# Experts' rows as 16-bit planes, packed by slot and transposed by DMA; low parts of expert weights on VectorE

## The chip, the cores and the metric

One core of a Trainium2 chip runs the whole program. The metric is device microseconds (us) of one execution, the median of a few runs. The core's engines are TensorE (PE in the rows; PEld is its weight load), VectorE (DVE), ScalarE (ACT), GpSimd (POOL) and SyncE (SP), which only issues DMAs here. Each engine works through its own instructions in a fixed order and waits where an operand is not there.

## The reference

A linear attention with a decaying state is followed by a gated two-matrix product and then by a mixture of experts. Only the last part is touched by the change, together with the step that hands rows to it.

```python
def _moe_ref(x, w1, w2, w3, w_out):            # 3072 tokens, 384 -> 1024 -> 384
    return ((x @ w1) * (x @ w2) @ w3) @ w_out

def _moe2_ref(x, w_gate, w_noise, noise, w1, w2):   # 8 experts, 384 -> 1024 -> 384
    logits = x @ w_gate
    noisy_logits = logits + np.log1p(np.exp(x @ w_noise)) * noise
    top2 = np.argpartition(-noisy_logits, 2, axis=1)[:, :2]
    ...                                        # softmax over the two
    for e in range(E):
        for k in range(2):
            mask = top2[:, k] == e
            h = np.maximum(x[mask] @ w1[e], 0.0)
            out[mask] += top2_w[mask, k, None] * (h @ w2[e])
```

## The kernel before

**Stages.** Up to about 110 us the weights of the dense part are folded and split. From there to about 470 us, twelve groups of two 128-token chunks go through attention and the dense part. From about 470 us to the end the eight experts follow one another. All matrix products use operands split into a high part (fp32r) and a low part (the rest), and take three matmuls each: high by high, high by low, low by high (`mm3`, L170 to L172).

**Rows and slots.** `mo_out` (L530 to L537) copies a chunk's 128 x 384 result from PSUM to the tile `xo` and writes it to the DRAM tensor `x2d` ("x_rows" in the rows). The gate (`gate_top`, `gate_put`) gives each token two slots of the DRAM table `slots`. An expert has 800 slots, in seven pieces: six of 128 rows and one of 32. The first four pieces are the first half (512 rows), the other three the second half (288 rows). `load_idx` (L718) reads an expert's slots into the tile `ti`, `gather` (L730) fetches the rows of a piece by an indirect DMA on GpSimd's queue into the tile `xg` (the 32 rows into `xgt`).

**Transposes.** The first matmul of an expert wants its rows with the 384 features on the partitions. `tr(e, hf)` (L734 to L742) makes that on TensorE: for each of three feature blocks, one transpose per piece (L739) into a PSUM bank, then `split` (L123, L124) casts the bank to the high part `XTh` on ScalarE and subtracts on VectorE to the low part `XTl`. A half of four pieces takes 12 transposes, one of three pieces takes 9.

**Weights.** `load_e` (L696) brings half of a weight matrix (768 KB) from DRAM to `raw` or `raww`; `split_e` (L699 to L709) casts a quarter on ScalarE to `WAh` or `WBh` and subtracts it to the low part `WAl` or `WBl`. The subtraction is on VectorE for experts 0 and 1 and on GpSimd from expert 2 on.

**Products.** `mm1(hf, ff)` makes eight blocks of the hidden layer per half (9 matmuls each), evicted by ScalarE (L754) and VectorE (L755). `mm2(e, j)` makes the output rows of a piece (24 matmuls, or 16 at L777 for the 32 rows), scales them on ScalarE (L772) and adds them to `out` by an indirect DMA on GpSimd's queue (L782).

**Order.** VectorE runs in the order in which the program is written (`manual_schedule`). On the other engines a scheduler may move an instruction ahead, except where `keep_in_program_order` stands. In the steady stretch, the second half of expert e also contains the weight quarters of expert e + 1 and both of its `tr`. At the last group of chunks (`g == NGRP - 1`) the first half of expert 0 begins before the gate of the last four chunks is done: its four pieces are gathered from the rows that stand so far (slots of 512 rows are held for that), and its `tr(0, 0)` stands ahead of the last piece of the dense part, of which VectorE still has to make the low part `pl` (L521). The gate's last chain (`LZ`, `g_t` to `g_si`) runs beside `mm1` of expert 0, and `tr(0, 1)` stands in the middle of the fourth `mm2` of expert 0.

Of the kernel before, what the change touches and what calls it, by code (L numbers as in the profile page):

```python
# [18 lines left out]
P = 128  # L19
# [52 lines left out]
def tile_kernel(ctx: ExitStack, tc: tile.TileContext, dt, nat, w3t, wout, w1, w2, e1, e2, cf, ci, out):  # L72
# [425 lines left out]

    def mo_ab(g, fp, m):
# [31 lines left out]
    def mo_out(g):  # L531
        for tt in range(2):
            t = 2 * g + tt
            dve.tensor_copy(out=LZ[:, t, :], in_=bX[tt][:, DM:XW])
            xo = work.tile([P, DM], F32, name="xo")
            act.copy(out=xo, in_=bX[tt][:, :DM])
            act.dma_start(out=x2d[DUMP + t * P:DUMP + P + t * P], in_=xo)  # L537
# [110 lines left out]
    def fill_table():  # L648
        ti = ic("init").rearrange("p (j t) -> p j t", t=2)
        tv = table.rearrange("(r s) t -> r s t", s=CAP)  # L650
        with nc.allow_non_contiguous_dma("table rows"):
# [5 lines left out]
            out=x2d[:DUMP].rearrange("(a p) d -> p a d", p=P), in_=zeros[:, None, :].to_broadcast([P, NT, DM])))  # L657
# [13 lines left out]
    def open_a():  # L671
# [3 lines left out]
        XT["t"] = EP["a"].tile([P, DM], F32, name="xgt")  # L675
        pool.memset(XT["t"], 0.0)
# [10 lines left out]
    def open_b():  # L687
        EP["b"] = ctx.enter_context(tc.tile_pool(name="epb", bufs=1, side="right"))
        open_h(EP["b"], 1)

    def load_e(e, m, i):
# [4 lines left out]
        sp.dma_start(out=rw, in_=(e1, e2)[m][e, :, 1536 * i:1536 * i + 1536])  # L696
        RW[e, m, i] = rw

    def split_e(e, m, i, on=pool):  # L699
# [5 lines left out]
        if e == 1:  # L705

            tc.keep_in_program_order(cast)
            on = dve
        on.tensor_tensor(out=l, in0=src, in1=f(h), op=OP.subtract)  # L709

    def load_idx(e, hf, r):
        TI[e, hf] = EP["a"].tile([P, (TA, TB + 1)[hf], 2], I32, name=f"ti{hf}", bufs=2)
        for o, n, w, j in (((0, TA, TPT, 0),), ((HOLD, TB, TPT, 0), (CAP - TPL, 1, TPL, TB)))[hf]:
            if isinstance(r, int):
                v = table[e * CAPT + r * CAP + o:e * CAPT + r * CAP + o + w * n]
            else:
                v = table[bass.ds(r * CAP + (e * CAPT + o), w * n)]
            sp.dma_start(out=TI[e, hf][:w, j:j + n].rearrange("p j t -> p (j t)"),  # L718
                         in_=v.rearrange("(p j) t -> p (j t)", p=w))
# [8 lines left out]
    def gather(e, j, rows=NROW):  # L728
        XG[e, j] = EP["a"].tile([P, DM], F32, name="xg", bufs=NT - 1) if j < NT - 1 else XT["t"]
# [12 lines left out]

    MB, MC, AD = (bA, bB, bK), [1], [-1]

# [14 lines left out]
    def mm2(e, j, mid=None):  # L759
# [4 lines left out]
        y = EP["a"].tile([P, DM], F32, name="ye", bufs=5)  # L764
# [31 lines left out]
    def second_half(e, r, early=True):  # L796

        nx = e + 1 < E
        if nx:
            for i in range(2):  # L800
# [231 lines left out]
```

## Time and profile before

| | |
|---|---|
| Median of 3 runs | 936.07 us (935.48 to 936.13) |
| The profiled execution | 935.5 us, its span in the trace 933.6 us |
| TensorE busy | 905.8 us (97%) |
| VectorE, ScalarE, GpSimd busy | 447.8, 423.4, 330.4 us |
| Transposes for the experts | 168, 21 per expert |
| DMA moved | 111.66 MB, mean 120 GB/s |

Each execution has some 2 us outside its span. The page's slices and the windows of the trace show which engine is busy when; the waits show who made TensorE wait; the timelines show the places where an operand comes late.

### The profile page before, as it was taken

The page shows a single profiled execution, that of the slowest core. Times are in us where ns is not written, and L with a number is a line of the kernel's source. Part 1 is how long each engine was busy: PE and PEld are TensorE (multiplying, and loading weights), DVE is VectorE, ACT ScalarE, POOL GpSimd, SP SyncE. Part 2 cuts the span into 40 slices and gives each one's busy share as a digit, 9 for nine tenths or more (in the row PEclk, how much of TensorE's full clock was granted, in tenths as well). Part 3 has the DMA queues.
Part 4 walks back from the last instruction along what each step waited for, and adds up shares of the span by engine and source line. Part 5 has one row for each costly group of instructions (what it writes and reads, how often), then busy time and mean ns, then how long its engine had stood idle before and what let it go on. Part 6 is the DMA issues. An engine that isn't in the chain of part 4 may idle for free.

```text
span 933.6 us, 17851 instructions
## 1 busy us (share of the span) xinstructions
PE 905.8 (97%) x7235; PEld 842.0 (90%) x7235; DVE 447.8 (48%) x1126; ACT 423.4 (45%) x875; POOL 330.4 (35%) x267
## 2 busy tenths in 40 slices
PE   8888899999999999999999999999999999999994
PEld 6778799999999999999989989899998989989894
DVE  5878875856756666655363451322313123131320
ACT  6877555456455545544351442434323343342420
POOL 2100111041141231230406626655546565555422
PEclk9999999999999999999999999999999999999998
DMA  9936577254353352400231635344162533614112
GB/s 356 405 121 226 187 80 216 89 141 159 105 156 128 117 147 81 119 19 19 84 121 39 158 118 164 59 145 89 40 169 62 161 62 94 140 29 105 18 21 37
DMA packets 52718, 111.66 MB, mean 120 GB/s; under 512 B 18064, under 2 KB 32656, under 8 KB 52624
## 3 DMA queue, kind: packets, MB, share of 16 engines
q1 hardware_dynamic: 37008, 85.98, 29.3%
q0 software_dynamic: 12160, 19.72, 12.0%
q10 hardware_dynamic: 3456, 4.72, 1.4%
q8 instruction: 58, 0.95, 0.4%
q14 instruction: 36, 0.29, 0.1%
HBM read 88.12 MB, written 22.27 MB: 118 GB/s over the span
## 4 chain that ended last, share of the span: by engine, by line
PE 87%; DVE 6%; ACT 3%; DMA 1%; issue 1%; POOL 0%; ACTq 0%; POOLq 0%; SPq 0%; DVEq 0%
PE pb L170 26%; PE pb L171 25%; PE pb L172 25%; PE pb L308 4%; PE pb L248 2%; PE pb L739 2%; PE pb L777 1%; PE pb L269 1%; PE pb L258 1%; DVE cvz L154 1%; ACT top L145 1%; DMA raw<-w 1%; ACT am L241 1%; DMA raw<-e 0%; PE pb L374 0%
## 5 line engine op out<-in xcount | busy, mean ns | idle before, releaser
L170 PE MATMUL pb<-XTh,WAh 128*128 128x512 f32 (+1 forms) x384 | 133.3, 348 | 0.0
L171 PE MATMUL pb<-XTl,WAh 128*128 128x512 f32 (+1 forms) x384 | 131.8, 343 | 0.0
L170 PE MATMUL pb<-WBh,HH 128*128 128x384 f32 x384 | 130.9, 341 | 0.0
L172 PE MATMUL pb<-XTh,WAl 128*128 128x512 f32 (+1 forms) x384 | 130.7, 343 | 0.0
L172 PE MATMUL pb<-WBh,HH 128*128 128x384 f32 x384 | 129.6, 337 | 0.0
L171 PE MATMUL pb<-WBl,HH 128*128 128x384 f32 x384 | 129.5, 337 | 0.0
L755 DVE SCALAR_TENSOR_TENSOR HH<-pb,HH 128x256 fp32r<-128x256 f32 (+1 forms) x128 | 71.3, 558 | 116.0 <-ACT HH L754 116.0
L782 POOL DMA_INDIRECT out<-ye,ti x56 | 87.3, 1559 | 107.5 <-ACT ye L772 94.3
L754 ACT ACTIVATE HH<-pb 128x256 fp32r<-128x256 f32 (+1 forms) x128 | 62.9, 493 | 124.7 <-PE pb L172 123.6
L642 POOL DMA_INDIRECT slots<-g_sc,g_si x48 | 52.4, 1091 | 159.4 <-DVE g_si L641 82.4
L772 ACT ACTIVATE ye<-pb,ti 128x384 f32<-128x384 f32 x48 | 28.0, 583 | 145.4 <-PE pb L172 129.7
L124 DVE TENSOR_TENSOR XTl<-pb,XTh 128x512 fp32r<-128x512 f32 (+1 forms) x48 | 25.2, 569 | 130.4 <-ACT XTh L123 130.4
L228 POOL TENSOR_TENSOR rku<-nrk 128x384 f32<-128x384 f32 x21 | 21.9, 1041 | 184.1 <-DVE cc L235 79.8
L170 PE MATMUL pb<-xh,WAh 128*128 128x256 f32 x288 | 82.0, 285 | 3.6 <-DVE W1l L124 3.1
L170 PE MATMUL pb<-xh,WBh 128*128 128x256 f32 x288 | 81.4, 283 | 1.6 <-ACT WAh L156 1.1
L171 PE MATMUL pb<-xl,WAh 128*128 128x256 f32 x288 | 82.0, 285 | 0.9 <-DVE xl L315 0.9
L172 PE MATMUL pb<-xh,WAl 128*128 128x256 f32 x288 | 82.0, 285 | 0.0
L172 PE MATMUL pb<-xh,WBl 128*128 128x256 f32 x288 | 81.4, 283 | 0.3 <-DVE WBl L161 0.3
L171 PE MATMUL pb<-xl,WBh 128*128 128x256 f32 x288 | 81.4, 283 | 0.0
L170 PEld LDWEIGHTS pb<-XTh,WAh 128*128 128x128 f32 x384 | 72.2, 188 | 9.6 <-DVE HH L755 1.5
L171 PEld LDWEIGHTS pb<-XTl,WAh 128*128 128x128 f32 x384 | 72.2, 188 | 8.0
L172 PEld LDWEIGHTS pb<-XTh,WAl 128*128 128x128 f32 x384 | 71.7, 188 | 8.2
(174 smaller groups left out, 2191.9 us busy)
## 6 DMA issues: line engine op xcount, KB each, us to landing
dtc<-dt SPq DMA_DIRECT2D x24, 772.0 KB, 5.0
raw<-e SPq DMA_DIRECT2D x18, 768.0 KB, 6.6
raww<-e SPq DMA_DIRECT2D x14, 768.0 KB, 4.4
nrk<-nat SPq DMA_DIRECT2D x24, 384.0 KB, 5.2
rawf<-w3t SPq DMA_DIRECT2D x16, 512.0 KB, 7.3
nv<-nat SPq DMA_DIRECT2D x24, 256.0 KB, 3.4
raw<-w SPq DMA_DIRECT2D x8, 768.0 KB, 4.9
out<-zeros SPq DMA_DIRECT2D x9, 576.0 KB, 4.5
```

The costliest lines, as they stand in the source:

```text
L124: (on or dve).tensor_tensor(out=l, in0=src, in1=f(h), op=OP.subtract)
L170: pe.matmul(o, wh, xh, start=start, stop=False)
L171: pe.matmul(o, wh, xl, start=False, stop=False)
L172: pe.matmul(o, wl, xh, start=False, stop=stop)
L228: on.tensor_tensor(out=t, in0=RK[j][:, :DM], in1=RK[j][:, DM:], op=OP.mult)
L248: pe.matmul(bST[hb][:, P * a:P * a + P], KT[j][q, a].rearrange("p s i -> p (s i)"), RT[j][q, a].rearrange("p s i -> p (s i)"), start=True, ...
L308: pe.matmul(o, lt, rh, start=st, stop=en, tile_position=tp)
L642: ins = pool.indirect_dma_start(out=table, out_offset=bass.IndirectOffsetOnAxis(ap=si[:, i, k:k + 1], axis=0), in_=SC[:, i, k, :], in_offs ...
L754: act.activation(out=Hh[hf][:, ff], in_=bank[:, :n], func=AF.Relu)
L755: dve.scalar_tensor_tensor(Hl[hf][:, ff], bank[:, :n], 0.0, f(Hh[hf][:, ff]), op0=OP.max, op1=OP.subtract)
L772: act.activation(out=y[:n], in_=bank[:n], func=AF.Copy, scale=wt)
L782: ins = pool.indirect_dma_start(out=out, out_offset=bass.IndirectOffsetOnAxis(ap=ti(e, j)[:, 0:1], axis=0), in_=y[:n], in_offset=None, com ...
```

## The change

Rows are written to `x2d` as two planes of 16-bit halves: for each token the 384 low halves, then the 384 high halves. `mo_out` makes the planes in its copy, which now moves 768 two-byte numbers in place of 384 four-byte ones. `gather` fetches such rows. A new function `turn(e, hf)`, on SyncE's queue, writes each gathered piece to a DRAM tensor `rows` (packed by slot, the two planes of a row one after the other) and then issues one DMA transpose from there to a tile `XTx` (`XTa` for expert 0), whose columns are read as 32-bit numbers again. `tr` becomes a cast on ScalarE and a subtraction on VectorE from that tile. Only the second half of expert 0 keeps its transposes on TensorE (`tr_pe`), after copies on VectorE that join the planes (`join`). All subtractions in `split_e` are on VectorE. Loads of weights and slots keep their written order on SyncE's queue. There are three slot tiles of each kind in place of two, seven `xg`, and six `ye`.

```diff
-    x2d = nc.dram_tensor("x2_rows", [NROW, DM], F32, kind="Internal").ap()
+    x2d = nc.dram_tensor("x2_rows", [NROW, 2 * DM], U16, kind="Internal").ap()
+    rows = nc.dram_tensor("expert_rows", [2, 2 * CAP, DM], U16, kind="Internal").ap()
...
-            act.copy(out=xo, in_=bX[tt][:, :DM])
+            act.copy(out=halves(xo), in_=bX[tt][:, :DM].bitcast(U16).rearrange("p (d t) -> p t d", t=2))
...
     def load_e(e, m, i):
...
-        sp.dma_start(out=rw, in_=(e1, e2)[m][e, :, 1536 * i:1536 * i + 1536])
+        tc.keep_in_program_order(sp.dma_start(out=rw, in_=(e1, e2)[m][e, :, 1536 * i:1536 * i + 1536]))
-    def split_e(e, m, i, on=pool):
+    def split_e(e, m, i):
...
-        if e == 1:
+        if e:
             tc.keep_in_program_order(cast)
-            on = dve
-        on.tensor_tensor(out=l, in0=src, in1=f(h), op=OP.subtract)
+        dve.tensor_tensor(out=l, in0=src, in1=f(h), op=OP.subtract)
...
+    def turn(e, hf):
+        for j in range(TA) if hf == 0 else range(TA, NT):
+            tc.keep_in_program_order(sp.dma_start(
+                out=rows[e % 2, 2 * TPT * j:2 * TPT * j + 2 * rows_of(j)].rearrange("(p t) d -> p (t d)", t=2),
+                in_=XG[e, j][:rows_of(j)]))
+        a = 2 * hf * NAB[0]
+        s = slice(a, a + 2 * NAB[hf])
+        tc.keep_in_program_order(sp.dma_start_transpose(out=XT["x"].bitcast(U16)[:, :, s], in_=rows[e % 2, s]))
     def tr(e, hf):
-        n = NAB[hf]
+        s = slice(hf * NAB[0], hf * NAB[0] + NAB[hf])
         for db in range(3):
-            bank = PB[4 + db]
-            for j in range(TA) if hf == 0 else range(TA, NT):
-                o = TPT * (j - hf * TA)
-                pe.transpose(bank[:, o:o + P], XG[e, j][:, P * db:P * db + P], ident)
-            s = slice(hf * NAB[0], hf * NAB[0] + n)
-            split(XT["h"][:, db, s], XT["l"][:, db, s], bank[:, :n])
+            x, h = XT["x"][:, db, s], XT["h"][:, db, s]
+            tc.keep_in_program_order(act.copy(out=h, in_=x))
+            dve.tensor_tensor(out=XT["l"][:, db, s], in0=x, in1=f(h), op=OP.subtract)
...
     def first_half(e, r):
         if e + 1 < E:
             need(e + 1, 0, r)
             need(e + 1, 1, r)
+            for i in range(2):
+                load_e(e + 1, 0, i)
         for ff in range(8):
             mm1(0, ff)
+            if ff in (3, 6) and e + 1 < E:
+                turn(e + 1, ff // 6)
+            if e == 1 and ff == 3:
+                tr(1, 1)
...
+            if g == NGRP - 1 and i == 7:
+                turn(0, 0)
             if g == NGRP - 1 and i == 11:
                 tr(0, 0)
...
-        mm2(0, j, (lambda: tr(0, 1)) if j == TA - 1 else None)
+        mm2(0, j, tr_pe if j == TA - 1 else None)
...
+    turn(1, 0)
+    turn(1, 1)
...
-        if j < NT - 1:
-            tr(1, j - TA)
+        if j == NT - 2:
+            tr(1, 0)
```

On SyncE's queue, where the first half of expert 0 is fetched, the slots of its four pieces (`ti_5911`) were followed by weight loads alone. This is before:

```order
L718 DMA ti_5911<-slots 128x8
L696 DMA raw_6080<-e 128x1536
L696 DMA raw_6082<-e 128x1536
L696 DMA raww<-e 128x1536 x2
L929 TENSOR_LOAD rounds
L929 ISA x2
L718 DMA ti_6352<-slots 128x4
```

The same place after the change:

```order
L720 DMA ti_5910<-slots 128x8
L701 DMA raw_5963<-e 128x1536
L738 DMA expert_rows<-xg 128x768 x4
L743 DMA_TRANSPOSE XTa<-expert_rows 128x3x1024
L701 DMA raw_6086<-e 128x1536
L965 TENSOR_LOAD rounds
L965 ISA x2
L720 DMA ti_6345<-slots 128x4
L720 DMA ti_6345<-slots 32x2
L701 DMA raww<-e 128x1536 x2
```

(`rounds` holds how many rounds of slots each expert needs.) Four writes and the transpose now stand between the two weight loads of expert 0, and the two loads for expert 1 (`raww`) moved behind the slots of expert 0's second half.

On ScalarE, after the last group's copies, the transposed rows of expert 0 are cast (`XTh`), and the rows of the last two chunks are copied (`xo`). Before:

```order
L123 CAST XTh<-pb_70 128x512
L514 CAST ph<-pp 128x512
L123 CAST XTh<-pb_71 128x512
L123 CAST XTh<-pb_72 128x512
L704 CAST WBh<-raw_6082 128x768 x2
L536 COPY xo<-pb_68 128x384
L537 DMA x_rows<-xo 128x384
L536 COPY xo<-pb_69 128x384
L552 ACTIVATE g_t<-g_t 128x32
```

After:

```order
L518 CAST ph<-pp 128x512
L749 CAST XTh<-XTa 128x512 x3
L708 CAST WBh<-raw_6086 128x768 x2
L540 COPY xo<-pb_68 128x768
L781 ACTIVATE HH_5860<-pb_66 128x512
L541 DMA x_rows<-xo 128x768
L540 COPY xo<-pb_69 128x768
L556 ACTIVATE g_t<-g_t 128x32
```

The first eviction of `mm1` (`HH`) now stands ahead of the gate's first function (`g_t`), and the copies are of 768 numbers.

On VectorE the place of the low part `pl` is the same in both: behind the three subtractions for expert 0. After the change they read the DMA's tile:

```order
L515 TENSOR_TENSOR pp<-ac,pb_67 128x512
L750 TENSOR_TENSOR XTl<-XTa,XTh 128x512 x3
L525 TENSOR_TENSOR pl<-pp,ph 128x512
L538 COPY LZ<-pb_68 128x16
L538 COPY LZ<-pb_69 128x16
L555 TENSOR_SCALAR g_t<-LZ 128x32
```

Before, the three subtractions were separate rows that read the banks `pb_70` to `pb_72`; nothing else moved there.

## Rows read from the trace of the kernel before

**Rows 1.** Page, part 1: busy us, share of the span, instructions.

```profile
PE 905.8 (97%) x7235; PEld 842.0 (90%) x7235; DVE 447.8 (48%) x1126; ACT 423.4 (45%) x875; POOL 330.4 (35%) x267
```

**Rows 2.** Windows: stretch, us; busy (count) PE, PEld, DVE, ACT, POOL; clock; DMA.

```profile
110.00:470.00 360.00, 357.66 (x3789) 346.38 (x3788) 223.90 (x627) 181.41 (x407) 87.10 (x83) 1.00 0.41 112
536.00:922.00 386.00, 385.49 (x2252) 352.91 (x2250) 106.78 (x234) 138.62 (x253) 202.44 (x137) 1.00 0.39 92
```

**Rows 3.** Waits of PE from 110 us on: total us, times, longest.

```profile
PE pb L171 <- DVE xl L315: 0.9, 1, 0.9
```

**Rows 4.** Chain that ended last, experts 1 and 2: start us, us, what.

```profile
584.54 1.31 PE pb L739 x12
590.02 0.98 PE pb L739 x9
...
640.00 1.31 PE pb L739 x12
```

**Rows 5.** Timeline of POOL, last of four gathers for expert 0's first half.

```profile
464.45 0.95 POOL L730 DMA_INDIRECT xg<-x_rows,ti  x1 [0.30 <-issue]
```

**Rows 6.** DMA: landing of those four gathers; issues over the whole span.

```profile
DMA to landing us min/median/max: 3.1/3.3/3.8
...
raww<-e SPq DMA_DIRECT2D x14, 768.0 KB, 4.4
...
x_rows<-xo ACTq DMA_DIRECT2D x24, 192.0 KB, 1.9
...
slots<-cit SPq DMA_DIRECT2D x1, 128.0 KB, 7.8
```

**Rows 7.** Timeline of PE where expert 0 begins: start us, us.

```profile
473.82 0.43 PE L170 MATMUL pb<-W1h,ph 128*128 128x400 f32 x1
...
476.84 0.45 PE L172 MATMUL pb<-W1h,pl 128*128 128x400 f32 x1
...
478.41 0.39 PE L170 MATMUL pb<-XTh,WAh 128*128 128x512 f32 x1
478.64 0.39 PE L171 MATMUL pb<-XTl,WAh 128*128 128x512 f32 x1
```

**Rows 8.** Timelines of ACT and DVE at the same place.

```profile
473.27 0.59 ACT L123 CAST XTh<-pb 128x512 fp32r<-128x512 f32 x1 [1.44 <-issue]
...
478.15 0.47 ACT L536 COPY xo<-pb 128x384 f32<-128x384 f32 x1
...
484.82 0.60 ACT L754 ACTIVATE HH<-pb 128x512 fp32r<-128x512 f32 x1 [0.94 <-PE pb L172]
...
478.61 0.17 DVE L534 COPY LZ<-pb 128x16 f32<-128x16 f32 x1 [0.55 <-PE pb L172]
...
485.26 0.68 DVE L755 SCALAR_TENSOR_TENSOR HH<-pb,HH 128x512 fp32r<-128x512 f32 x1
```

**Rows 9.** Expert 0's second half: last gather, first transpose; gathers' landing from 529 to 541 us.

```profile
507.35 0.87 POOL L730 DMA_INDIRECT xgt<-x_rows,ti  x1 [0.30 <-issue]
...
510.39 0.38 PE L739 MATMUL pb<-cft,xg 128*128 128x128 f32 x2
...
DMA to landing us min/median/max: 5.4/6.1/6.7
```

**Rows 10.** Expert 1: last gather of its first half, first matmul.

```profile
514.32 0.96 POOL L730 DMA_INDIRECT xg<-x_rows,ti  x1 [0.30 <-issue]
...
535.15 0.48 PE L170 MATMUL pb<-XTh,WAh 128*128 128x512 f32 x1
```

**Rows 11.** Windows, columns as in rows 2: a wait of PE at 67 us, and after.

```profile
67.00:70.00 3.00, 0.06 (x1) 0.00 (x0) 2.28 (x5) 1.94 (x5) 0.77 (x2) 1.00 0.55 173
70.00:73.40 3.40, 3.20 (x15) 3.20 (x16) 3.06 (x7) 2.74 (x6) 0.00 (x0) 0.50 0.56 191
```

**Rows 12.** Instructions on `raww`: ns min, median, max; first and last start.

```profile
L704 ACT CAST WAh<-raww x28: 817/832/869, 527.8 to 840.1; 128x768 fp32r<-128x768 f32 x28
...
L709 DVE TENSOR_TENSOR WAl<-raww,WAh x4: 934/954/959, 528.7 to 537.9; 128x768 fp32r<-128x768 f32 x4
```

More of the change, by code (lines that the diff above doesn't have):

```diff
@@ L497, in tile_kernel, with halves @@
     PH, PL, AC, LOWP = {}, {}, {}, []
+    def halves(x):
+        return x.rearrange("p (t d) -> p t d", t=2)
     def mo_ab(g, fp, m):
@@ L534, in mo_out @@
             dve.tensor_copy(out=LZ[:, t, :], in_=bX[tt][:, DM:XW])
-            xo = work.tile([P, DM], F32, name="xo")
-            act.copy(out=xo, in_=bX[tt][:, :DM])
+            xo = work.tile([P, 2 * DM], U16, name="xo")
+            act.copy(out=halves(xo), in_=bX[tt][:, :DM].bitcast(U16).rearrange("p (d t) -> p t d", t=2))
             act.dma_start(out=x2d[DUMP + t * P:DUMP + P + t * P], in_=xo)
@@ L656, in fill_table @@
         tc.keep_in_program_order(sp.dma_start(
-            out=x2d[:DUMP].rearrange("(a p) d -> p a d", p=P), in_=zeros[:, None, :].to_broadcast([P, NT, DM])))
+            out=x2d[:DUMP].rearrange("(a p) d -> p a d", p=P), in_=zeros.bitcast(U16)[:, None, :].to_broadcast([P, NT, 2 * DM])))
     def fill_out(i):
@@ L689, in open_b @@
         open_h(EP["b"], 1)
+        XT["x"] = EP["b"].tile([P, 3, CAP], F32, name="XTx")
     def load_e(e, m, i):
@@ L717, in load_idx @@
                 v = table[bass.ds(r * CAP + (e * CAPT + o), w * n)]
-            sp.dma_start(out=TI[e, hf][:w, j:j + n].rearrange("p j t -> p (j t)"),
-                         in_=v.rearrange("(p j) t -> p (j t)", p=w))
+            tc.keep_in_program_order(sp.dma_start(out=TI[e, hf][:w, j:j + n].rearrange("p j t -> p (j t)"),
+                                                  in_=v.rearrange("(p j) t -> p (j t)", p=w)))
     def rows_of(j):
@@ L728, in gather, with join, tr_pe @@
     def gather(e, j, rows=NROW):
-        XG[e, j] = EP["a"].tile([P, DM], F32, name="xg", bufs=NT - 1) if j < NT - 1 else XT["t"]
+        XG[e, j] = EP["b" if e else "a"].tile([P, 2 * DM], U16, name="xg", bufs=NXG)
         pool.indirect_dma_start(out=XG[e, j][:rows_of(j)], out_offset=None, in_=x2d[:rows],
                                 in_offset=bass.IndirectOffsetOnAxis(ap=ti(e, j)[:, 0:1], axis=0))
-    def tr(e, hf):
-        n = NAB[hf]
+    def turn(e, hf):
[6 more added lines that the diff above has]
+        tc.keep_in_program_order(sp.dma_start_transpose(out=XT["x"].bitcast(U16)[:, :, s], in_=rows[e % 2, s]))
+    def tr(e, hf):
+        s = slice(hf * NAB[0], hf * NAB[0] + NAB[hf])
+        for db in range(3):
+            x, h = XT["x"][:, db, s], XT["h"][:, db, s]
+            tc.keep_in_program_order(act.copy(out=h, in_=x))
+            dve.tensor_tensor(out=XT["l"][:, db, s], in0=x, in1=f(h), op=OP.subtract)
+    def join(j):
+        x = EP["a"].tile([P, DM], F32, name="xg", bufs=NXG)
+        dve.tensor_copy(out=x[:rows_of(j)].bitcast(U16).rearrange("p (d t) -> p t d", t=2),
+                        in_=halves(XG[0, j][:rows_of(j)]))
+        XG[0, j] = x
+    def tr_pe():
+        for j in range(TA, NT):
+            join(j)
+        s = slice(NAB[0], NAB[0] + NAB[1])
         for db in range(3):
             bank = PB[4 + db]
-            for j in range(TA) if hf == 0 else range(TA, NT):
-                o = TPT * (j - hf * TA)
-                pe.transpose(bank[:, o:o + P], XG[e, j][:, P * db:P * db + P], ident)
-            s = slice(hf * NAB[0], hf * NAB[0] + n)
-            split(XT["h"][:, db, s], XT["l"][:, db, s], bank[:, :n])
+            for j in range(TA, NT):
+                n, o = rows_of(j), TPT * (j - TA)
+                pe.transpose(bank[:, o:o + n], XG[0, j][:n, P * db:P * db + P], ident[:n, :n])
+            split(XT["h"][:, db, s], XT["l"][:, db, s], bank[:, :NAB[1]])
     MB, MC, AD = (bA, bB, bK), [1], [-1]
+    NXG = 7
     def mm1(hf, ff, banks=None):
@@ L798, in second_half @@
         nx = e + 1 < E
-        if nx:
-            for i in range(2):
-                load_e(e + 1, 0, i)
         for ff in range(8):
@@ L809, in second_half @@
                 split_e(e + 1, 0, j)
-            if nx and j in (4, 5):
-                tr(e + 1, j - 4)
+            if nx and j in (3, 5):
+                tr(e + 1, j // 5)
         if nx:
@@ L920, in one_expert @@
         for hf in range(2):
+            turn(e, hf)
             tr(e, hf)
```

14 lines of the change are left out of this document (7 added, 7 removed).

## The prediction

> **What bounds the kernel now.** I read the page's busy times first: TensorE is busy for 905.8 us of the span of 933.6 us, and no other engine for half of it [rows 1]. The windows then show where. From 110 to 470 us it is busy for 357.7 of 360 us, and in the experts' steady stretch, 536 to 922 us, for 385.5 of 386 us at full clock, with VectorE at 106.8 us [rows 2]. The waits agree: from 110 us on TensorE was made to wait three times only, 0.9 us at the longest [rows 3]. So from 110 us on the time is the sum of TensorE's work. What is taken off it is gained whole, and any wait that the change puts ahead of it is paid whole.
>
> **The transposes removed.** The chain gives 1.31 us for the 12 transposes of a first half and 0.98 us for the 9 of a second half, 109 ns each [rows 4]. Expert 0 loses 12, experts 1 to 7 lose 21 each: 159 in all, 159 x 0.109 = **17.3 us off TensorE**. The 9 of expert 0's second half stay. An expert's period is 640.00 - 584.54 = 55.46 us [rows 4], and should be 55.46 - 2.29 = 53.2 us.
>
> **The price of a DMA transpose.** The trace has none, so I bound D, the time of the one for 1,024 x 384 two-byte numbers (786 KB). From below: as many bytes as a weight load of 768 KB, 4.4 us [rows 6]. From above: a DMA in small pieces. The table fill of 128 KB goes out as 4,096 pieces of 32 bytes and lands after 7.8 us, 1.9 ns a piece [rows 6]. If the transpose moves 128 numbers of a row at a time (its shape is 3 blocks of 128 columns), it has 3,072 pieces: 5.9 us. In pieces of 32 bytes it would have 24,576: 47 us. I take 6.5 us, near the piece count of whole blocks and the load of equal size, with a little for the weight load beside it. The second half's (576 rows) takes 0.56 of that.
>
> The Trainium skill, "DMA: Bandwidth & Descriptors", section "Latency and other measured facts", gives 261 GB/s for a DMA transpose; my estimate from that page, with the 2 us of fixed cost that it states for any DMA, is D = 5.0 us. No run here shows it yet. With it the first wait below would be 1.3 us and the whole 1.5 us shorter.
>
> **Steady stretch: hidden.** For experts 2 to 7 `turn` is issued in the first half of the expert before, and its result is wanted after that expert's fourth `mm2`, more than 35 us later. Both transposes take 1.56 D = 10 us and the six writes that matter 1.9 us each [rows 6], so this cover holds for D up to about 25 us. `turn` on SyncE's queue has the next `raw` loads behind it, which wait for the 32-row matmuls of the same expert anyway. GpSimd loses its 48 subtractions; VectorE gets them at 0.954 us [rows 12], 8 per expert, 46 us more in a stretch of 386 us where it has 106.8 [rows 2]: 40% busy, at the places where expert 1 had them on VectorE before. I charge nothing. `xo` copies grow from 0.47 us to about 0.83 us, as a cast of 768 numbers takes [rows 8, 12]; ScalarE is half idle there [rows 2]. Nothing again.
>
> **Expert 0's first half: a new wait.** Here there is no cover. The last gather is issued at 464.45 and lands 3.1 to 3.8 us later [rows 5, 6], at about 467.8. The write behind it takes 1.9 us [rows 6] and its issue some 0.3: the transpose starts at 470.0 and is done at 470 + D. From the first `XTh` cast to the first matmul that uses `pl` it took 476.84 - 473.27 = 3.6 us [rows 7, 8], and the order still puts `pl` behind the three subtractions. So that matmul can run at 473.6 + D. TensorE's other work lasts until then thus: the 16 matmuls that stood between 473.82 and 476.84 [rows 7] start 1.3 us sooner and end at 475.5; eight matmuls of `mm1`, now ahead of `pl`, add 8 x 0.23 (478.64 - 478.41, rows 7) = 1.8: 477.3. The wait is D - 3.7: **2.8 us** at D = 6.5, 0.7 at 4.4.
>
> **The gate's last chain.** From the last `LZ` copy to the end of VectorE's first eviction were 485.94 - 478.61 = 7.3 us [rows 8]. ScalarE now has an eviction (0.60) ahead of `g_t` and two copies longer by 0.36: 7.3 + 1.3 = 8.6 us, ending 10.1 us after `pl` (eight matmuls of 0.18 come before `LZ`). TensorE has those eight and 28 of 0.23 ahead of the bank that it wants: 7.9. **2.2 us** of waiting; 0.9 if the 1.3 are hidden, 3 if more stands in line.
>
> **Expert 0's second half.** Its last gather is issued at 507.35, and TensorE transposed at 510.39 [rows 9], nearly at once. Now the two `raww` loads are issued just ahead of the gathers, and beside such loads gathers land after 5.4 to 6.7 us [rows 9]; then comes a `join` copy of 768 numbers, 0.83 to 0.95 us by the nearest rows [rows 12]. With 3.1 us to land the wait would be 1.0, with 6.7 us 4.6. The loads are half done when the gathers begin: **2.2 us**.
>
> **Expert 1's first half.** Two scatters now precede its gathers where one did, so the last is issued 1.9 us after 514.32 [rows 10], lands by 519.7, is written by 522, and transposed at 522.2 + D. It is wanted 1.3 us (cast and subtraction) ahead of 535.15 [rows 10] - 2.3 + 2.2 = 535.0. The wait is D - 11.6: **none** at 6.5.
>
> **Sum.** -17.3 + 2.8 + 2.2 + 2.2 = -10.1 us. The profiled execution took 935.5 us, its span and 1.9 around it, 0.6 below the median 936.07. 935.5 - 10.1 = 925.4, and set against the median 926.0. I say **926.0**.
>
> **The clock.** At 67 us TensorE stood still for 3 us at full clock, and from 70.0 to 73.4 us the granted clock was 0.50, the lower of its two levels of 1.2 and 2.4 GHz [rows 11]: 1.7 us lost. A new wait of over 3 us may bring the same once more. At 2.8 us I charge nothing; each longer wait costs 1.7.
>
> **Rivals.**
> - *A slower transpose, still a gain.* D from 9 to 13 us: at 11 the first wait is 7.3, the others 4.4, the clock 1.7: 13.4 against 17.3, about **932**. For it: 256-byte pieces from DRAM may cost more than 1.9 ns. Against it: the table's pieces are smaller.
> - *The transpose becomes the bound: slower than before.* All rests on D, and the point is D = 14 (10.3 + 4.4 + 2.4 + 1.7 = 18.8 is over 17.3). At D = 20 the waits are 16.3 + 4.4 + 8.4 and the clock 3.4: 32.5 - 17.3 = +15, **951**. If its 24 blocks of 128 x 128 went one after the other, each at the 1.9 us of a small DMA [rows 6], D would be 46, both together 71 us would exceed the period of 53.2 six times, and the kernel would need over 1,000 us. For it: nothing in the trace shows such a DMA. Against it: the loads and writes of the same bytes are quick.
> - *The cover moves, no gain.* VectorE, with its order fixed, holds the evictions back in the second half and TensorE waits 2 us per expert again: **935**. For it: eight more subtractions per expert in a fixed order. Against it: expert 1 ran so before, without a wait of TensorE [rows 3].
>
> The Trainium skill, "VectorE: DVE Perf Modes", section "The three transpose paths", gives 1309 ns for a 128 x 128 block by DMA against 390 ns on TensorE, and its rules advise TensorE where the result may lie in PSUM. It speaks against this change: if its blocks add up one by one, my estimate is D = 24 x 1.309 = 31 us and a time near 974. The trace here has TensorE at 109 ns a block, below the page's figure, and no DMA transpose.
>
> **How the numbers follow.** The forecast's case (D below 9, waits as above) has 0.66, the slower transpose 0.13, the transpose as bound 0.16, no gain 0.05. The forecast's own range is 920 to 931: at its fast end D = 4.4 and the lower bounds, 0.7 + 0.9 + 1.0 = 2.6, give 921.4, and I leave a microsecond for waits that don't come. For 8 in 10 the range must take in the slower transpose and the point where it turns: 919.5 to 937. A measurement of this kernel can tell about 0.2% (1.9 us) from no change. Faster by more than that: 0.66 + 0.13 = 0.79. Within it: 0.06, the case without gain and a hundredth of the bound's. Slower: 0.15.
>
> **What would show it.** In the changed profile: 9 transposes of TensorE in place of 168; a period of 53.2 us between experts, with no wait of TensorE in it; the landing of the DMA transposes (4.4 to 9 us); one wait of TensorE near 475 us for `XTh` or `pl`, one near 486 us for the gate or a bank, one near 511 us for `join`. The forecast is wrong if the transpose lands after more than 9 us, if waits recur in each expert, or if the clock falls in the experts.

## The result, and the profile of the changed kernel

The changed kernel takes **943.83 us** (median of 5 runs, 940.41 to 946.05), the kernel before beside it 936.13 us (5 runs, 935.48 to 939.2): a ratio of 1.0070, 95% interval 1.0053 to 1.0088. It is slower by 0.7%, and the forecast was 926.0 us, faster. The profiled execution took 944.25 us, its span 942.5 us, so 8.9 us more than before.

The page's busy times, as in [rows 1]: us, share of the span, instructions.

```profile
PE 902.0 (96%) x7076; PEld 834.2 (89%) x7076; DVE 493.0 (52%) x1177; ACT 429.6 (46%) x875; POOL 243.6 (26%) x218
```

The windows over the two stretches of [rows 2], moved to where they now lie; same columns (busy us and count of PE, PEld, DVE, ACT, POOL; clock; DMA).

```profile
112.40:472.40 360.00, 357.66 (x3788) 346.39 (x3788) 223.89 (x627) 187.93 (x407) 86.58 (x82) 1.00 0.43 119
546.70:930.20 383.50, 376.18 (x2128) 342.71 (x2128) 151.39 (x285) 137.90 (x254) 117.72 (x91) 0.99 0.54 133
```

The 159 transposes are gone (7235 - 7076 matmuls). VectorE is busy for 45 us more, where 46 were forecast, and GpSimd for 87 us less. The dense stretch is the same to a hundredth. But the second stretch, where TensorE was idle for 0.5 us before, has 7.3 us of idle time and a mean clock below 1. The waits of TensorE say for whom (total us, times, longest):

```profile
PE pb L171 <- ACT XTh L749: 9.9, 3, 6.6
...
PE pb L766 <- DVE xg L754: 1.8, 3, 1.4
...
PE pb L173 <- DVE pl L525: 1.0, 2, 0.6
...
PE pb L171 <- DVE HH L782: 0.6, 1, 0.6
```

None of these but `pl` was there before [rows 3]. Three waits on `XTh` make 9.9 us; the longest alone is 6.6 us. It lies in expert 1, at the first matmul of its second half. Timelines of TensorE and of ScalarE (start us, us, what, in brackets the idle time before it and who ended it):

```profile
568.44 0.61 PE L171 MATMUL pb<-XTh,WAh 128*128 128x288 f32 x1 [6.62 <-ACT XTh L749]
```

```profile
544.78 0.58 ACT L799 ACTIVATE ye<-pb,ti 128x384 f32<-128x384 f32 x1 [3.06 <-issue]
545.26 0.82 ACT L708 CAST WAh<-raww 128x768 fp32r<-128x768 f32 x1
545.98 1.66 ACT L749 CAST XTh<-XTx 128x512 fp32r<-128x512 f32 x3
...
567.96 1.10 ACT L749 CAST XTh<-XTx 128x288 fp32r<-128x288 f32 x3 [6.64 <-DMA XTx<-expert_rows]
```

ScalarE stood for 6.64 us until a DMA transpose into `XTx` had landed. Which one, the queue of SyncE tells:

```profile
531.42 4.54 SPq L743 DMA_TRANSPOSE XTx<-expert_rows  x1
536.06 1.50 SPq L738 DMA_DIRECT2D expert_rows<-xg  x3
539.07 1.46 SPq L743 DMA_TRANSPOSE XTx<-expert_rows  x1
...
562.73 3.11 SPq L743 DMA_TRANSPOSE XTx<-expert_rows  x1
```

Expert 1's own halves were issued at 531.42 and 539.07; the second landed after 5.8 us, at 544.86, 17 us before it was wanted. The transpose that ended the wait is the one of 562.73, and that is **expert 2's** first half. The chain of waits gives its length: 5.15 us, to 567.88.

```profile
562.73 5.15 DMA XTx<-expert_rows
567.96 0.44 ACT XTh L749
568.44 0.61 PE pb L171
```

At three of these places the clock fell as well. Windows, columns as above, the clock the third last:

```profile
478.50:481.20 2.70, 1.54 (x6) 1.06 (x7) 1.79 (x3) 1.66 (x3) 0.00 (x0) 1.00 0.66 255
481.25:484.70 3.45, 3.45 (x11) 3.15 (x10) 0.84 (x3) 2.09 (x3) 0.00 (x0) 0.51 0.00 0
518.80:525.60 6.80, 6.80 (x24) 5.95 (x25) 1.37 (x3) 1.78 (x4) 5.28 (x6) 0.50 0.78 162
561.80:563.10 1.30, 0.02 (x1) 0.00 (x0) 0.00 (x0) 0.00 (x0) 0.00 (x0) 1.00 0.04 14
563.20:573.40 10.20, 4.96 (x15) 4.27 (x16) 3.26 (x6) 1.48 (x4) 0.00 (x0) 0.50 0.69 164
573.40:600.00 26.60, 26.60 (x169) 24.44 (x169) 11.44 (x26) 9.82 (x18) 6.55 (x5) 1.00 0.37 99
```

Three falls to the lower level (1.2 of 2.4 GHz): 3.4, 6.8 and 10.2 us long. The first two begin behind a wait, the last 1.4 us into the wait of 6.62 us, and in that one the engine worked for only 4.96 us. Half of the busy time in a fall is lost: about 1.7, 3.4 and 2.5 us, and the 2.5 comes on top of the 6.6 us of waiting.

The steady stretch did what was forecast. First matmuls of experts 2 and 3:

```profile
610.53 0.39 PE L171 MATMUL pb<-XTh,WAh 128*128 128x512 f32 x1
...
663.87 0.40 PE L171 MATMUL pb<-XTh,WAh 128*128 128x512 f32 x1
```

That is a period of 53.34 us against 55.46 [rows 4].

**Where the time went, place by place.** The same instructions were looked up in each trace, and their starts compared with the kernel before. From each difference the one at the last dense group (448.7 us of before) is taken off: it is 2.4 us in the changed kernel, between -1.6 and +3.2 in the runs below, and 1.7 in one whose code is unchanged up to there, so it is no effect of the change. An output tile is one `mm2`; the times in brackets are those of the kernel before. The columns e1 to e14 are experiments of the next section; e14 is the changed kernel mended at four places.

| lag in us behind the kernel before, at | changed kernel | e1 | e2 | e5 | e10 | e13 | e14 |
|---|---|---|---|---|---|---|---|
| expert 0, third output tile (508.5) | 3.2 | 4.1 | 3.7 | 1.1 | 0.5 | 0.4 | 3.2 |
| expert 0, fourth output tile (513.7) | 8.7 | 9.1 | 8.7 | 7.1 | 4.9 | 1.9 | 4.6 |
| expert 0, 32-row tile (528.6) | 7.8 | 7.9 | 7.6 | 5.8 | 3.6 | 0.6 | 3.3 |
| expert 1, 32-row tile (566.0) | 19.6 | 11.8 | 9.3 | 16.9 | 2.9 | 2.5 | 3.0 |
| expert 7, 32-row tile (898.8) | 6.4 | -1.4 | -3.9 | 3.5 | -10.1 | -10.7 | -10.0 |

The changed kernel loses 3.2 us in expert 0's first half, 5.5 at the transposes of its second half, and 11.7 in expert 1; from there to expert 7 it gains 13.2 us, 2.2 an expert.

### The profile page after: what moved, and what is told of

Its sections match the earlier page's. It is cut to its first block, busy times and chain, and to the rows that moved or that the text cites. A ratio compares the mean times of both kernels' runs of the same rounds, so it can differ in the third digit from the quotient of the medians.

```text
span 942.5 us, 17579 instructions
## 1 busy us (share of the span) xinstructions
PE 902.0 (96%) x7076; PEld 834.2 (89%) x7076; DVE 493.0 (52%) x1177; ACT 429.6 (46%) x875; POOL 243.6 (26%) x218
## 4 chain that ended last, share of the span: by engine, by line
PE 78%; DVE 6%; issue 6%; DMA 5%; ACT 2%; POOL 2%; POOLq 0%; SPq 0%; DVEq 0%; ACTq 0%
PE pb L171 23%; PE pb L172 23%; PE pb L173 23%; PE pb L309 3%; PE pb L249 2%; DMA ti<-slots 1%; PE pb L804 1%; PE pb L270 1%; POOL slots L646 1%; DVE cvz L155 1%; PE pb L259 1%; DMA xg<-x_rows,ti 1%; ACT top L146 1%; DMA raw<-w 1%; POOL xg L732 1%
## 5 line engine op out<-in xcount | busy, mean ns | idle before, releaser
L781 ACT ACTIVATE HH<-pb 128x512 fp32r<-128x512 f32 (+1 forms) x128 | 62.8, 492 | 120.4 <-PE pb L173 118.8
L171 PEld LDWEIGHTS pb<-WBh,HH 128*128 128x128 f32 x384 | 72.6, 189 | 5.9 <-ACT WAh L708 4.4
L242 ACT ACTIVATE am<-cft,cc 128x128 f32<-128x128 f32 x192 | 61.2, 393 | 29.9 <-DVE cc L236 29.9
```

The costliest lines, as they stand in the source:

```text
L171: pe.matmul(o, wh, xh, start=start, stop=False)
L242: act.activation(out=AM[j][:, h], in_=ident, func=AF.Copy, scale=KS["c", j][:, h:h + 1])
L781: act.activation(out=Hh[hf][:, ff], in_=bank[:, :n], func=AF.Relu)
```

## The experiments

Ratios are to the kernel before on the same chip, with their 95% interval. Its median differed from chip to chip, 935.9 to 941.3 us, so runs of different groups are compared by ratio.

### e1: one call moved by a line

```diff
-            if ff in (3, 6) and e + 1 < E:
-                turn(e + 1, ff // 6)
             if e == 1 and ff == 3:
                 tr(1, 1)
+            if ff in (3, 6) and e + 1 < E:
+                turn(e + 1, ff // 6)
```

> The changed kernel, with expert 1's second-half casts (the call tr(1, 1) in its first half) written ahead of turn(2, 0) instead of behind it; nothing else. Theory 1 (shared tile): the cast that held the PE for 6.6 us at 561.8 waits for the DMA transpose of expert 2's first half, issued 562.73 and landed 567.88, because both halves lie in one tile XTx and are tracked as one, though its own rows had landed at 544.86. Then the wait goes, and with it the 10.2 us at clock 0.5 behind it (5.1 us of work): about 943.8 - 6.6 - 5.1 = 932 us, no PE wait over 1 us between 550 and 600, no clock fall there. Theory 2 (expert 1's own transpose is slow, or the queue behind it is): the wait stays at 4 us or more, 940 to 944 us. Theory 3 (the shared tile makes the wait, but the clock falls there anyhow): 937 us.

Measured 932.68 us (before 936.31), ratio 0.9955 (0.9939 to 0.9971): 11.2 us less than the changed kernel, theory 1's number. The parts of that theory were not quite so: of the 5.1 us for the clock the windows above leave 2.5, and by the traces the lag at expert 1 falls by 7.8 us here and by 10 in e2 (this run's profiled execution has a fall of its own at 549.8, 1.7 us). The wait of 6.6 us and the fall behind it are gone. What stays of `XTh` in the waits of TensorE is 4.3 us at two places, the starts of experts 0 and 1:

```profile
PE pb L171 <- ACT XTh L749: 4.3, 2, 2.3
```

So the cast waited for a transfer that it does not read, because it stood behind that transfer in the program and both use the tile `XTx`.

### e2: two tiles

```diff
-        XT["x"] = EP["b"].tile([P, 3, CAP], F32, name="XTx")
+        XT["x0"] = EP["b"].tile([P, 3, NAB[0]], F32, name="XTx0")
+        XT["x1"] = EP["b"].tile([P, 3, NAB[1]], F32, name="XTx1")
...
```

> The changed kernel with the tile XTx cut in two, one for each half of an expert's rows, order unchanged. Theory 1 (shared tile): both false waits go, the 6.6 us one at 561.8 and the 1.96 + 0.35 us one at 544.7 (the casts of expert 1's first half, which wait on the transpose of its second half, landed 544.86), with the clock fall behind the first (5.1 us): about 943.8 - 6.6 - 5.1 - 2.0 = 930 us, that is 2 us below the run with the order swapped. Theory 2 (slow transposes): 940 to 944 us, and waits on the transposes stay at both places. If the wait at 544.7 stays while the other goes, its own transpose (issued behind the first half's gathers, landing about 544) is late by itself, and the time is that of the swapped order, 932 us.

Measured 931.92 us (before 936.31), ratio 0.9951 (0.9931 to 0.9971). The order is that of the changed kernel and the 6.6 us are gone all the same: it was the shared tile. But the second wait, which I had put down to the same cause, did not move (TensorE, then ScalarE, then the landing of expert 1's first transpose, issued at 530.91):

```profile
544.29 0.73 PE L171 MATMUL pb<-XTh,WAh 128*128 128x512 f32 x2 [1.96 <-ACT XTh L750]
```

```profile
542.42 0.58 ACT L800 ACTIVATE ye<-pb,ti 128x384 f32<-128x384 f32 x1 [3.06 <-issue]
542.90 0.82 ACT L709 CAST WAh<-raww 128x768 fp32r<-128x768 f32 x1
543.62 1.66 ACT L750 CAST XTh<-XTx 128x512 fp32r<-128x512 f32 x3
```

```profile
XTx<-expert_rows SPq DMA_TRANSPOSE x1, 6.0
```

The data were there at 536.9. The casts came at 543.6 because ScalarE's fixed order has them behind the last `ye`, which waits for TensorE itself. My expectation for "the wait stays" (a late transpose) was wrong as well.

### e6: the casts one tile earlier

```diff
-        if j == NT - 2:
+        if j == NT - 1:
             tr(1, 0)
```

This kernel and e7, e8 and e10 to e14 have the two tiles; e5 has the one tile of the changed kernel.

> The changed kernel with XTx in two tiles, and expert 1's first casts (the call tr(1, 0)) written one tile of expert 0's second product earlier. In the run with two tiles alone the PE still waited 1.96 + 0.34 us at 544.3, although its transpose had landed at 536.90: on ScalarE the casts stood behind the `ye` of 542.42, which waits for the PE's last tile, and one cast of weights. Theory A (ScalarE's order makes this wait): it goes, 2 to 2.5 us less than 931.9, so 929.5 us, and no PE wait over 0.5 us within 10 us of expert 1's start. Theory B (the transpose's data or VectorE's subtractions are late there): the wait stays over 1 us and the time at 931 to 932 us.

Measured 935.15 us on a chip where the kernel before takes 941.33 us: ratio 0.9934 (0.9906 to 0.9962). The interval takes in e2's ratio, so the time alone does not decide. The trace does: between 535 and 570 us TensorE waits for nothing, and from expert 0's 32-row tile to expert 1's the lag falls by 0.7 us where it rose by 1.7 in e2. Theory A, 2.4 us.

On this chip the kernels also lose 2 to 7 us between expert 0's fourth and fifth output tile, where those of the other chips don't. ScalarE stands there in a place that no edit touched, and the trace names no instruction of the core that it waited for. In e8:

```profile
527.34 0.38 ACT L782 ACTIVATE HH<-pb 128x256 fp32r<-128x256 f32 x1 [4.16 <-remote]
```

e9, whose code there is that of before, shows it too (2.0 us). Its cause was not sought.

### e5 and e7: the gate's low part ahead of expert 0's first casts

```diff
             if g == NGRP - 1 and i == 11:
+                low_p()
                 tr(0, 0)
```

> The changed kernel, with the gate's low-part piece of the last group written ahead of expert 0's first casts (the call tr(0, 0)) instead of behind them, so that the gate's chain on VectorE does not queue behind the low parts that wait for the first DMA transpose. Theory 1: the waits at 478.1 (1.3 us) and 491.9 (0.37 + 0.61 us) shrink by 1 to 2 us together, and if the fall to half clock at 481.25 (3.4 us, 1.7 us of work) goes with them, 3 to 4 us: 940 to 942 us. Theory 2: the wait at 478.1 is the transpose's own landing, which no order of VectorE changes: the time stays within 1 us of 943.8.

Measured 940.90 us (before 936.31), ratio 1.0041 (1.0025 to 1.0057): 2.9 us less than the changed kernel. The timeline of TensorE from 474 to 520 us has the wait on `XTh` no longer, only 0.23 us on `XTl`, then the gate and the joins:

```profile
486.68 0.18 PE L600 MATMUL pb<-g_mb,trib 128*128 128x32 bf16 x1 [1.52 <-DVE g_mb L584]
513.72 3.06 PE L766 MATMUL pb<-cft,xg 128*128 128x128 f32 x9 [2.07 <-DVE xg L754]
```

and the clock stays whole from 478 to 486 us:

```profile
478.00:486.00 8.00, 7.15 (x30) 5.62 (x31) 3.98 (x25) 6.55 (x11) 0.00 (x0) 1.00 0.19 69
```

At the third output tile the lag is 1.1 us instead of 3.2. The wait was not the transfer's alone: eight matmuls of the dense part's last piece now fill it, since their low part no longer queues behind three subtractions that wait for the transfer. But most of the wait has only moved to the gate: 0.23 + 1.52 us are left of 1.30 + 0.23 + 0.37 + 0.61. The larger part of the gain is the fall of the clock that is missing here, 1.7 us, and e14 below, with the same edit, has one.

e7 has this edit on top of e6.

> As the run before it, with the gate's low-part piece ahead of expert 0's first casts as well. Theory A: the two places are independent, so the 2.9 us that this order gave by itself (940.9 against 943.8) comes on top: 926.5 us, with no wait on XTh at expert 0's start, no fall to half clock near 480, and the wait on the joins near 512 left. Theory B (the time won at the gate is waited for again at the gathers behind it): 929 us or more, and the waits near 512 are longer by what was won.

Measured 933.85 us (before 941.33), ratio 0.9910 (0.9890 to 0.9930); 0.9910 x 936.2 = 927.8, between the two theories. The trace is on A's side: at the third output tile the lag is 0.6 us against 4.3 in e6, and at the fourth, behind the joins, 5.6 against 10.2, so what is won at the gate is not waited for again there. By expert 0's 32-row tile 2.9 us of it are left, since this run stood longer at the place on ScalarE named under e6.

### e4: VectorE's share alone

```diff
-        if e == 1:
+        on = dve
+        if e:
             tc.keep_in_program_order(cast)
-            on = dve
```

> The kernel before, with one part of the change alone: the low parts of all experts' weights are subtracted on VectorE and none on GpSimd, the casts kept in program order. Theory 1 (VectorE has room in the steady stretch, the loss lies with the transposes): within 2 us of 936.1. Theory 2 (VectorE's extra 45 us of work delays what the PE needs): 940 us or more, with PE waits on VectorE in each expert.

Measured 937.73 us (before 936.31), ratio 1.0007 (0.9994 to 1.0020): theory 1. The window that [rows 2] shows has VectorE at 150.8 us instead of 106.8, and TensorE does not stand still in it:

```profile
536.00:922.00 386.00, 386.00 (x2258) 353.57 (x2257) 150.79 (x283) 136.72 (x254) 115.69 (x90) 1.00 0.39 93
```

### e9: waits of known length

```diff
...
+    def hold(k):
+        l = Hl[0][:, 0:6, :P]
+        dve.scalar_tensor_tensor(l[:, 0], MB[7 % 3][:, :P], 0.0, f(l[:, 0]), op0=OP.mult, op1=OP.add)
+        for _ in range(k):
+            dve.tensor_copy(out=l, in_=f(l))
...
+        if e in HOLD_E:
+            hold(HOLD_E[e])
```

> The kernel before, with the PE held at four places where it never waits: ahead of the second product of experts 2, 3, 4 and 5, by VectorE operations that rewrite an operand with its own values (one after the last matmul of the first product, then 0, 1, 3 and 6 copies of 128x768). It prices a wait by its length. Theory A (a wait costs its own length, as the prediction charged it): the period from one expert to the next grows by the wait alone, and the granted clock stays at 1.0 behind the waits. Theory B (the clock falls behind a wait, as at the four waits of the changed kernel): the granted clock is 0.5 for 3.4, 6.8 or 10.2 us behind each, and each costs 1.7 to 5.1 us beyond its own length, more behind longer ones.

Measured 958.56 us in one run. The two short holds made no wait: the 32-row tile was scheduled into their place. The two long ones did, and they differ. Windows around the wait of 2.14 us (745.35) and around the one of 3.92 us (806.82):

```profile
742.80:745.30 2.50, 0.41 (x2) 0.00 (x0) 2.46 (x2) 0.61 (x2) 2.08 (x1) 1.00 1.01 410
745.35:750.00 4.65, 4.12 (x22) 3.80 (x22) 0.00 (x0) 0.45 (x1) 0.00 (x0) 1.00 0.98 396
802.50:806.80 4.30, 0.40 (x2) 0.00 (x0) 4.13 (x5) 0.60 (x2) 2.07 (x1) 0.85 0.99 406
806.80:812.30 5.50, 5.48 (x17) 5.48 (x18) 0.00 (x0) 0.00 (x0) 0.00 (x0) 0.50 0.56 219
```

After 2.14 us the clock stays at 1.00. With the wait of 3.92 us it falls to 0.50 for 6.8 us in all: the last 1.3 us of the wait and 5.5 us behind it, of which half, 2.7 us, are lost. The hold of 3.92 us cost its expert 8.4 us of period: 3.9 of waiting, 0.7 of a second wait behind it, 2.7 of clock, and 1.1 that is not assigned. The hold of 2.14 us cost 5.2 us, with 2.9 us of waiting and no fall, so a period here prices a wait only roughly: matmuls also changed places around the holds. Neither theory holds alone. In the changed kernel a fall followed waits of 1.30 and 1.45 us, and none followed the 1.96 us at the start of expert 1. That same wait of 1.96 us stands in e1 and e5 too, and there a fall of 3.4 us follows it (at 549.8 and 544.4), while in e2 none does. So the length of the wait does not decide it by itself. What else does is left open.

### e8, e10, e12, e13, e14: the rest of expert 0

e8 writes the loads of `raww` later in the program, on top of e7.

```diff
         if j == 0:
-            load_e(1, 0, 0)
-            load_e(1, 0, 1)
             need(1, 0, 0)
+        if j == 2:
+            load_e(1, 0, 0)
+            load_e(1, 0, 1)
```

> As the run before it, with the two loads of expert 1's first weights issued behind expert 1's first index load, after the third tile of expert 0's second product instead of the first, so that expert 0's second gathers do not share the DMA engines with them. Theory A (the loads slow the index load, 3.4 us against 2.3 us in the kernel before, and the gathers, 2.9 to 4.6 us against 2.6 to 3.1 us): the wait on the joins (2.0 + 0.4 us) shrinks by 1.5 to 2.4 us and, if the fall to half clock behind it goes too, by 1.7 us more: 923 to 925 us. Theory B (the joins' own 1.8 us on VectorE and the transpose order make the wait): within 1 us of the run before.

Measured 933.0 us (before 941.33), ratio 0.9910 (0.9893 to 0.9927), theory B's number. But the loads left at 506.05, with the gathers at 508.32: SyncE has nothing to wait for there, so a later place in the program is not a later time. The run says nothing on the loads.

e10 undoes the change for expert 0 alone: each 128 tokens' rows are written a second time as 32-bit rows, and expert 0's are gathered from there and transposed on TensorE, on top of e6.

```diff
+            xf = work.tile([P, DM], F32, name="xf")
+            act.copy(out=xf, in_=bX[tt][:, :DM])
+            act.dma_start(out=x32[DUMP + t * P:DUMP + P + t * P], in_=xf)
...
-        pool.indirect_dma_start(out=XG[e, j][:rows_of(j)], out_offset=None, in_=x2d[:rows],
+        pool.indirect_dma_start(out=XG[e, j][:rows_of(j)], out_offset=None, in_=(x2d if e else x32)[:rows],
...
-                turn(0, 0)
...
-                tr(0, 0)
+                tr_pe(0)
```

> The changed kernel with XTx in two tiles and the earlier first casts of expert 1, and the change undone for expert 0 alone: its rows are kept a second time as 32-bit rows in DRAM (one ScalarE copy and one write more for each 128 tokens), gathered from there and transposed on the PE, 21 transposes. Theory A (what is left of the loss lies in expert 0, where nothing hides the transposes, while experts 1 to 7 save 2.2 us each): expert 0 takes what it took before, and the time is 936.2 - 7 x 2.2 = 921 us on a chip where the kernel before takes 936.2 us, a ratio of 0.984, 0.978 to 0.988. Theory B (the lag of expert 0 comes from the DMA traffic or from the weights' splits, which stay): the waits near 490 and 515 stay, the ratio is that of the runs before, 0.991 to 0.995. Theory C (the second copy of the rows costs in the dense stretch): the groups' starts fall behind those of the kernel before by more with each group.

Measured 925.97 us (before 935.85), ratio 0.9898 (0.9878 to 0.9918): between A and B. The first half's lag is gone (0.5 us at the third output tile), and the dense groups keep their pace, so not C. But 4.5 us are lost again at the second half's transposes, now with no join in the way. TensorE waits for the gathers themselves, and the clock falls; their median landing is 5.0 us, where the kernel before had 2.6 to 3.1 at this place:

```profile
PE pb L768 <- DMA xg<-x_rows,ti: 1.8, 1, 1.8
```

```profile
xg<-x_rows,ti POOLq DMA_INDIRECT x3, 5.0
```

```profile
508.00:512.80 4.80, 2.94 (x16) 2.02 (x15) 0.24 (x1) 0.52 (x2) 3.92 (x3) 1.00 0.91 260
512.80:516.20 3.40, 3.40 (x12) 3.12 (x11) 1.14 (x3) 0.68 (x2) 2.76 (x3) 0.50 0.81 139
```

e12 is e10 with e8's edit.

> As the run before it, with the two loads of expert 1's first weights issued after the third tile of expert 0's second product. If these loads slow expert 0's second gathers there as well: 1 to 3 us less than the run before it. If the PE transposes, which need no joins, leave the gathers enough room: within 0.7 us.

Measured 928.45 us (before 935.85), ratio 0.9912 (0.9894 to 0.9930): the loads left at 507.2, beside the gathers, as in e8. Again it tells nothing on them.

e13 and e14 move the loads ahead of expert 0's second index load, which waits for the gate. e13 is e10 with this edit, e14 is e7 with it (planes for expert 0 too).

```diff
     open_b()
+    load_e(1, 0, 0)
+    load_e(1, 0, 1)
     load_idx(0, 1, 0)
...
         if j == 0:
-            load_e(1, 0, 0)
-            load_e(1, 0, 1)
             need(1, 0, 0)
```

> The run with expert 0 on the PE (transposes of 32-bit rows), with the two loads of expert 1's first weights written ahead of expert 0's second index load, where the kernel before has them on SP's queue. In the run with them after the third tile they still left at 507 us, beside the gathers: SP had nothing to wait for, so that edit moved nothing, and it tells nothing on these loads. Theory A (the loads slow the gathers beside them, 5.9, 5.0 and 3.9 us to landing against 3.0, 3.1 and 2.6 us in the kernel before): the gathers land in about 3 us, the PE's wait of 1.8 us at 511 and the fall to half clock behind it go, 3 us or more less than the 925.97 us of that run at a kernel before of 935.85 us, a ratio of 0.985 to 0.987. Theory B (the gathers are slow there for another reason): the ratio stays at 0.990.

> All rows as planes, XTx in two tiles, the earlier first casts of expert 1, the gate's low-part piece ahead of expert 0's first casts (the run that came to a ratio of 0.991), and the loads of expert 1's first weights early as in the run beside it. Theory A (they slow the gathers): the wait on the joins near 512 (2.0 us) shrinks by 1.5 us or more, ratio 0.987 to 0.989. Theory B (the joins alone make that wait): ratio 0.991. If this run and the one beside it come out equal, the 32-bit rows for expert 0 buy nothing once the loads are early.

e13 measured 923.94 us (before 938.65), ratio **0.9847** (0.9826 to 0.9868); e14 926.19 us (before 938.65), ratio 0.9884 (0.9858 to 0.9911). Theory A in both. In e13 the loads leave at 484, the gathers land in 3.1 us, TensorE waits 0.6 us for them, and the clock stays whole:

```profile
xg<-x_rows,ti POOLq DMA_INDIRECT x3, 3.1
```

```profile
PE pb L768 <- DMA xg<-x_rows,ti: 0.6, 2, 0.4
```

```profile
508.00:513.00 5.00, 4.44 (x26) 3.96 (x24) 0.00 (x0) 0.58 (x1) 3.78 (x5) 1.00 0.31 90
```

The loss between the third and the fourth output tile is 1.5 us in both runs, 4.5 in e10 and 5.5 in the changed kernel. So the loads made it, and the joins cost next to nothing once the gathers are early (0.32 + 0.18 us of waiting in e14). In the changed kernel itself the gathers are slowed less than in e10: they land after 4.4, 3.6 and 2.6 us (3.0, 3.1 and 2.6 before). But the first is issued only 1.8 us ahead of the third tile's `ye`, where it was 3.7 us before; in e14 it is 2.7. How much of that the loads cause is not shown.

Whether the 32-bit rows buy anything beyond e14 is open: the intervals overlap, and at expert 7 the lags are -10.7 and -10.0 us. The table shows why they come out so near. In e14 the wait of TensorE for the gate has a fall of the clock behind it (0.50 from 488.4 to 491.9):

```profile
487.21 0.18 PE L600 MATMUL pb<-g_mb,trib 128*128 128x32 bf16 x1 [1.70 <-DVE g_mb L584]
```

Waits of 1.52 us in e5 and 1.44 us in e7 at this matmul had none. e13 has no such wait, but in expert 1 TensorE waits 2.29 us at 547.1 for an eviction on VectorE, and its lag grows there. Both are faster than the kernel before, and than the changed one; e13, by 1.5%, is the fastest that was measured.

### e11: each transpose three times

```diff
+        for _ in range(3 if e > 1 else 1):
...
```

> The changed kernel with XTx in two tiles and the earlier first casts of expert 1, and each DMA transpose of experts 2 to 7 issued three times in a row into the same place: the transfer becomes about three times as long (5.2 us to some 15 us). The prediction held that from expert 2 on some 25 us of other work cover it. Theory A (covered): the period from expert to expert stays at 53.3 us, with no PE wait over 0.5 us on XTh. Theory B (the cover is small): the period grows, by 10 us if nothing covers it.

Measured 949.17 us in one run. It is neither theory: the periods from expert 2 to 7 are 53.4, 59.3, 53.3, 57.1 and 54.7 us. The first halves, now 19 to 24 us from the first issue to the last landing, are hidden in every expert. The three of the second half come behind them on the queue; where the last lands after ScalarE has reached its casts, its evictions of the next expert queue behind them. TensorE then waits, over the whole run five times (the first, 0.6 us, before expert 2):

```profile
PE pb L171 <- DVE HH L784: 12.5, 5, 6.1
```

ScalarE and TensorE at 654 us:

```profile
654.12 1.10 ACT L751 CAST XTh<-XTx 128x288 fp32r<-128x288 f32 x3 [3.95 <-DMA XTx<-expert_rows]
```

```profile
656.55 0.79 PE L171 MATMUL pb<-XTh,WAh 128*128 128x512 f32 x1 [2.90 <-DVE HH L784]
```

The clock falls for 6.8 us at this place, which with the wait makes the 5.9 us by which that period is longer. So the cover is real, and it is used up at about three times the present length.

## Why the prediction was wrong

- **The price of the transpose: right.** D was 6.5 us, by bounds 4.4 to 47. The chain gives 5.15 us for expert 2's; in e2 the first halves of experts 1 to 7 land after 5.3 to 7.9 us, 5.9 in the middle, and the slowest in e13 after 9.8. The Trainium skill, "DMA: Bandwidth & Descriptors", section "Latency and other measured facts", with its 261 GB/s had led to an estimate of 5.0 us: the 5.15 us agrees, most of the others are longer. The Trainium skill's 1309 ns a block, "VectorE: DVE Perf Modes", section "The three transpose paths", does not add up block by block here: 24 blocks took 5.15 us, 215 ns each, and 410 ns each at the slowest.
- **Transposes removed and the steady stretch: right.** 159 are gone, the period is 53.34 us (forecast 53.2), and experts 2 to 7 gain 13.2 us. VectorE's added work costs nothing that e4 can tell, and ScalarE's longer copies nothing in the dense stretch (357.66 us busy of 360, as before). The bound of 25 us for D does not follow from the prediction's own terms, since 1.56 D and six writes of 1.9 us, one after another, fill 35 us at D = 15. In e11, with 19 to 24 us for the first halves, TensorE waits, so the 974 us given for D = 31 are too low by such waits.
- **Expert 0's first half and the gate: near in sum, by luck.** 2.8 and 2.2 us were forecast. With D = 5.15 the prediction's own D - 3.7 is 1.5 us, and the trace has 1.30 + 0.23; the gate's two waits are 0.37 + 0.61. That is 2.5 us, half of the 5.0, and 1.7 us of clock, which nobody had charged, came on top: 4.2 us, less 1.3 for the 12 transposes, about the 3.2 us of the table.
- **Expert 0's second half: the wait right, the clock missing.** 2.2 us were charged, between bounds of 1.0 and 4.6, and TensorE waited 1.45 + 0.18 + 0.21 = 1.8; with 3.4 us of clock the place cost 5.5. The cause was named, `raww` beside the gathers, and e13 bears it out.
- **Expert 1: the step that failed and turned the sign.** "The wait is D - 11.6: none" looked only at when the data land. It left out two things that the order of the code holds: the casts stand on ScalarE behind a `ye` that waits for TensorE (2.4 us by e6), and in the second half `tr(1, 1)` stands behind expert 2's `turn(2, 0)`, which writes the same tile. For that second half the prediction has no step at all, so its wait stood at nothing. It measured 6.6 us and 2.5 us of clock; by the traces the place cost 10 us (against e2), by the medians 11.2 (against e1). "Steady stretch: hidden" was true of expert 2's transpose itself; what it holds up in expert 1 was not asked.
- **The clock: charged nothing, wrong.** Three falls, at waits of 1.30, 1.45 and 6.62 us, lost some 1.7 + 3.4 + 2.5 us. The rule taken from [rows 11], that only a wait of over 3 us brings one, was one sighting. A fall of the clock in the experts was among the prediction's own signs of being wrong.

Put together by the traces, from the forecast's -10.1 us: +10.0 (shared tile, its clock with it), +2.4 (casts behind `ye`), +3.3 (second half), -0.5 (3.2 in the first half against 5.0 - 1.3) and +0.5 (13.2 for the steady stretch against 6 x 2.29 = 13.7) give +5.6, against 6.4 at expert 7 in the table; the last 0.8 is not assigned. None of the rivals was this one; the third, a fixed order that holds something back, came nearest, but on VectorE and in every expert.

## What to carry to other kernels

When a transfer is moved ahead, ask what it writes and who, later in the program, touches the same tile: here a reader of another part of that tile waited for it as well, and a tile for each half or a call one line earlier took that away. (Shown for a DMA transpose into a part of a tile; other writes were not tried.) A fixed order on an engine has to be read entry by entry at the seams (first and second expert here), where the steady stretch's cover does not exist yet. And a load moves in time only if its place on its queue is ahead of, or behind, something that waits.

## What was not expected of the hardware

The clock fell after waits of TensorE as short as 1.30 us (3.4 us at 0.50), while waits of 1.96 and 2.14 us at other places passed without a fall; and one and the same wait of 1.96 us brought a fall in two kernels (e1, e5) and none in two others. Beside two loads of 768 KB three gathers took 5.0 us in the median (e10), with the loads moved away 3.1 us (e13). On one of the chips the kernel before itself took 941.3 us against 935.9 on another. The kernel before was not traced there; in the kernels that were, ScalarE stands in expert 0 for a source that the trace does not name.
